# First attention of a fused attention and expert kernel: one VectorE product for both heads, inverse sums in a shared PSUM bank, and k copies moved from ScalarE to VectorE

## The chip, the cores and the metric

The kernel runs on one core of one Trainium2 chip. The metric is the time of the device in microseconds (us), from start to end of one execution, as the median of several runs. The engines are TensorE (PE, with its weight loads as PEld), VectorE (DVE), ScalarE (ACT), GpSimd (POOL) and SyncE (SP), which here only issues DMAs. [...]

## The reference

Attention with global and local keys over 4 batches of 8 heads, 768 positions and 64 columns per head, followed by a mixture of 4 experts over the 3072 rows:

```python
scores = scale * np.matmul(q, k.transpose(0, 1, 3, 2))
scores = scores + bias[None]                 # -slope * distance, per head
scores = np.where(keep, scores, -1e9)        # first 8 keys, and the last 96
a = np.exp(scores - max); a = a / (a.sum(-1) + 1e-9)
x = np.matmul(a, v)                          # rows: 4 * 768, columns: 8 * 64
p = domain_probs / (domain_probs.sum(-1) + 1e-9)
for e in range(4):
    out += p[:, e:e+1] * (np.maximum(x @ w1[e], 0) @ w2[e])
```

## The kernel before

The attention of batch 0 comes first and alone ("first attention", `attention_early`, pools made with `early=True`). The experts of batch 0 then run on PE while the attention of the next batches is woven in, and so on to the end. The change touches the first attention only; the code for the later attention (`early=False`) keeps its form.

The first attention works on four pairs of heads, in the order 0, 2, 1, 3. A pair has six tiles of 128 query rows, so there are 24 tiles, and each call of `flow` (a *step*, numbered 0 to 27 here) takes in one new tile and moves the tiles before it one stage on. For step n the stages are:

- PE: the scores of tiles n and n+1, in even steps, into two PSUM tiles `ps0` and `ps1` (one per head, both tiles beside each other in each);
- DVE and ACT, tile n-1 (`one` in the code): per head, DVE adds the bias and takes the maximum out of PSUM into `pb` (the CUSTOM instruction), and ACT takes the exponential and its row sum `zsum`;
- DVE, tile n-2 (`two`): adds 1e-9 to the two row sums between the two heads of tile n-1, inverts them after the second head (RECIPROCAL), and multiplies `pb` by them, one instruction per head (TENSOR_SCALAR_CACHE_REDUCE, an accumulating form whose sum goes to `spare` and is not used; each is followed by a short READ_ACCUMULATOR);
- PE and ACT, tile n-3: `turn` transposes the scaled `pb` into a PSUM tile `pt`, and ACT copies it to `pT`;
- PE and ACT, in steps 6, 9, 12, ... 27: `weigh` multiplies three turned tiles with v into the PSUM tile `px`, with 20 matmul instructions for tiles 0 to 2 of a pair and 24 for tiles 3 to 5, and ACT copies `px` to `x`.

The first tile of each pair has 128 columns per head, the others 256. After a step, `AHEAD` says whether one more part of a next pair is prepared: three PE transposes of half of q or k into `pt`, and one ACT copy of 384 columns out of it (`prepare_early`). For the last three pairs the k halves come after steps 4, 5, 8, 9, 13 and 14, the q halves after 3, 6, 7, 10, 12 and 15. After the first half of k POOL copies its first 32 columns beside every tile. After steps 17 to 20 DVE has one sum of x blocks each for the experts (`first_sums`, tiles named xB in the trace). After step 25 PE runs a first product of the experts (`opening`, into a `ps` tile), which reads x of the last pair's first half.

All engines take their instructions in the order of the program in this stage (`Ordered.on`), so that an instruction that waits holds up all that is behind it on its engine. Waits follow from the tiles that instructions read and write. [...]

Of the kernel before, what the change touches and what calls it, by code (L numbers as in the profile page):

```python
# [9 lines left out]
F32 = mybir.dt.float32  # L10
# [3 lines left out]
AF = mybir.ActivationFunctionType  # L14
ALU = mybir.AluOpType
# [3 lines left out]
P = 128  # L19
# [167 lines left out]
def attn_moe_kernel(ctx: ExitStack, tc, q, k, v, n_global, n_local, domain_probs, w1, w2, out):  # L187
# [9 lines left out]
    HALF = S // 2  # L197
# [12 lines left out]
    ve, ac, po, sy, te = (Ordered(tc, e) for e in (nc.vector, nc.scalar, nc.gpsimd, nc.sync, nc.tensor))  # L210

    PAIRS = (0, 2, 1, 3)
# [116 lines left out]
    def transpose_half(A, nat, hf):  # L329
        tp = A.pt.tile([P, 512], F32, name="pt")  # L330
        for t in range(TPH):
            te.transpose(tp[:, t * P : (t + 1) * P], nat[:, hf * TPH + t].rearrange("p j d -> p (j d)"), ident)
        return tp
# [30 lines left out]
        if hf == 0:  # L364
            ve.tensor_copy(kd[:, :, :, P:], f32(kd[:, :, 0:1, :NGLOB]).to_broadcast([P, 2, NQT, NGLOB]))

    def prepare_early(A, nat, hf, name, got):

        tp = transpose_half(A, nat, hf)
        tpv = tp[:, :HALF].rearrange("p (t c) -> p t c", c=P)  # L370
        pl = slice(hf * TPH, (hf + 1) * TPH)
        if name == "q":
            if hf == 0:
                got["q"] = A.qd.tile([P, NQT, P], F32, name="early_q")
            ac.activation(got["q"][:, pl, :], tpv, AF.Copy, scale=-SCALE)
            return
        if hf == 0:
            got["k"] = A.kd.tile([P, NQT, PL], F32, name="early_k")
        dst = got["k"]
        ac.copy(dst[:, pl, :P], tpv)  # L380
        if hf == 0:
            po.tensor_copy(dst[:, :, P:], dst[:, 0:1, :NGLOB].to_broadcast([P, NQT, NGLOB]))

# [36 lines left out]
    def softmax(A, new, old):  # L420


        if old:
            pb, zsum = old["pb"], old["zsum"]
        if new:
            t, pr, ps = new["t"], new["pr"], new["ps"]
            cols = slice(0, P) if t == 0 else slice(0, 2 * P)
            bcol = slice(2 * P, 3 * P) if t == 0 else slice(0, 2 * P)
            new["pcol"] = pcol = slice(P, 2 * P) if t == 0 else slice(0, 2 * P)
            nmax = A.small.tile([P, 2], F32, name="nmax")  # L430
            new["zsum"] = A.small.tile([P, 2], F32, name="zsum")
            new["pb"] = A.pb.tile([P, 2, 2 * P], F32, name="pb")
        for j in range(2):
            if new:
                e = new["pb"][:, j, pcol]
                ve.tensor_tensor_reduce(
                    e, ps[j][:, cols], nbias[:, 2 * pr + j, bcol], 1.0, 3.0e38, ALU.add, ALU.min, nmax[:, j : j + 1]
                )
                ac.activation(
                    e, e, AF.Exp, bias=nmax[:, j : j + 1], scale=-1.0, accum_out=new["zsum"][:, j : j + 1]  # L440
                )
            if old:
                if j == 1:
                    ve.reciprocal(zsum, zsum)
                elif A.early:

                    old["spare"] = spare = A.small.tile([P, 3], F32, name="spare")
                    ve.tensor_scalar(zsum, zsum, 1e-9, None, op0=ALU.add, op1=ALU.add, accum_out=spare[:, 2:3])
                else:
                    ac.activation(zsum, zsum, AF.Copy, bias=1e-9)  # L450
        if old:
            for j in range(2):
                p = pb[:, j, old["pcol"]]
                if A.early:
                    ve.tensor_scalar(
                        p, p, zsum[:, j : j + 1], None, op0=ALU.mult, op1=ALU.add, accum_out=old["spare"][:, j : j + 1]
                    )
                else:
                    ac.activation(p, p, AF.Copy, scale=zsum[:, j : j + 1])

    def turn(A, tile_):

        t, pb = tile_["t"], tile_["pb"]
        pt = A.pt.tile([P, 2, 2, P], F32, name="pt")
        pT = A.pT.tile([P, 2, 2, P], F32, name="pT")
        w0 = 1 if t == 0 else 0
        for w in range(w0, 2):
            for j in range(2):
                te.transpose(pt[:, w, j, :], pb[:, j, w * P : (w + 1) * P], ident)
        ac.copy(pT[:, w0:], pt[:, w0:])  # L470
        tile_["pT"] = pT

    def weigh(A, three, x, b):

        px = A.px.tile([P, 512], F32, name=A.pxname)
        for i, tile_ in enumerate(three):
            t, pr, pT = tile_["t"], tile_["pr"], tile_["pT"]
            vt, vg = tile_["v"]["v"], tile_["v"]["vg"]
            for w in range(1 if t == 0 else 0, 2):
                for j in range(2):  # L480
                    vv = vt[:, j, t] if w == 1 else vg[:, j, t - 1]
                    te.matmul(
                        px[j * D : (j + 1) * D, i * P : (i + 1) * P],
                        vv,
                        pT[:, w, j, :],
                        start=(w == 1 if t == 0 else w == 0),
                        stop=(w == 1),
                    )
        cols = slice((t - TPH + 1) * P, (t + 1) * P)
        if x is not None:  # L490
            ac.copy(x[:, pr, cols], px[:, :HALF])
        else:
            piece = A.st.tile([P, HALF], F32, name="piece")
            ac.copy(piece, px[:, :HALF])
            ac.dma_start(xd[b][:, pr, cols], piece)
# [3 lines left out]
    def attention_early(A):  # L499

        b = 0
        x = xs[b] = xp.tile([P, NPAIR, S], F32, name="x")
        tiles, turned, ahead = [None] * 4, [], [None]

        def flow(new=None):

            one, two, three, four = tiles
            if new:
                if new["t"] % 2 == 0:
                    new["ps"], ahead[0] = scores_early(A, new["t"], gots[new["pr"]])  # L510
                else:
                    new["ps"] = ahead[0]
            if four:
                turned.append(four)
            softmax(A, one, two)
            if three:
                turn(A, three)
            if len(turned) == TPH:
                weigh(A, turned, x, b)
                turned.clear()  # L520
            tiles[:] = [new, one, two, three]

        def start(pr):

            nats[pr] = {n: next(load(A, src, b, pr, n)) for n, src in (("q", q), ("k", k), ("v", v))}

        def prepare_all(pr):

            nat, got = nats[pr], gots[pr]
            got["v"] = nat  # L530
            prepare_early(A, nat["q"], 0, "q", got)
            if pr:
                yield 1
            prepare_early(A, nat["k"], 0, "k", got)
            yield 1
            nat["vg"] = windows(A, nat["v"])
            prepare_early(A, nat["k"], 1, "k", got)
            yield 1
            prepare_early(A, nat["q"], 1, "q", got)
            yield 1  # L540

        nats, gots = {}, [{} for _ in range(NPAIR)]
        halves = [load(A, src, b, 0, n, 2) for n, src in (("q", q), ("k", k))]
        bias = biases(start_stack.enter_context(tc.tile_pool(name="setup", bufs=1)))
        next(bias)
        nats[0] = dict(zip(("q", "k"), (next(h) for h in halves)))
        for h in halves:
            next(h)
        nats[0]["v"] = next(load(A, v, b, 0, "v"))
        todo = [prepare_all(pr) for pr in PAIRS]  # L550
        next(bias)
        next(todo[0])
        start(PAIRS[1])
        for m, pr in enumerate(PAIRS):
            cur = gots[pr]
            for t in range(NQT):
                if t == 2 and m + 2 < NPAIR:
                    start(PAIRS[m + 2])
                flow({"t": t, "pr": pr, **cur})
                if (m, t) in BIASES:  # L560
                    next(bias)
                for _ in range(AHEAD[m][t]):
                    while todo and next(todo[0], 0) == 0:
                        todo.pop(0)
                yield
        while any(tiles):
            flow()
            yield
# [281 lines left out]
    late = []  # L850
# [119 lines left out]
    with ExitStack() as start_stack:  # L970
        A = Pools(start_stack, "start", st=1, kd=2, qd=2, nat=2, natv=3, pb=4, ps=2, pt=3, px=1, early=True)
# [11 lines left out]
    op = main.enter_context(tc.tile_pool(name="op", bufs=1))  # L983
# [3 lines left out]
    A = Pools(  # L987
        att_stack, "att", st=1, kd=1, qd=2, nat=1, natv=1, pb=2, ps=2, pt=2, px=0, early=False, side="right"
    )
# [463 lines left out]
```

## Time and profile before

| | us |
|---|---|
| median of 3 runs | 1165.45 (1165.42 to 1165.84) |
| profiled execution, its own time | 1164.69 |
| its span in the profile | 1162.9 |
| busy in the span: PE / DVE / ACT / POOL | 1140.5 / 853.2 / 618.2 / 606.6 |
| PEclk over the span | 0.999 of full speed |
| last copy of x of the first attention starts | 59.98 |

The profile counts times from the start of the span. A row of the timeline gives the start, the duration, the engine and the tiles written and read; where one instruction starts before the one ahead of it has ended, the distance from start to start is what it costs its engine.

### The profile page before, as it was taken

To read this page: it belongs to the slowest core of one execution; us is meant where nothing else is said; L and a number is where in the kernel's file an instruction comes from. 1 tells how busy PE (TensorE), PEld (TensorE's weight loads), DVE (VectorE), ACT (ScalarE), POOL (GpSimd) and SP (SyncE) were. 2 spreads that over 40 slices of the span, in tenths; PEclk is the share of its full clock that TensorE was granted. 3 is DMA by queue.
4 is the path that set the end of the run, shared out by engine and by line. 5 is a ranking of instruction groups with operands and counts; after the bars stand their busy time and mean duration, and the time that the engine had idled before them with its cause. 6 is when DMAs were issued, how large, how long until landed. Compare 5 with 4: busy or idle time off the path is not lost.

```text
span 1162.9 us, 21146 instructions
## 1 busy us (share of the span) xinstructions
PE 1140.5 (98%) x7474; PEld 1062.6 (91%) x7474; DVE 853.2 (73%) x1944; ACT 618.2 (53%) x1597; POOL 606.6 (52%) x592
## 2 busy tenths in 40 slices
PE   7899999999999999999999999999999999999997
PEld 5678898989888989899998899999999999999997
DVE  7977776767767777776776777777777777777776
ACT  6854767777653665655565334444445444444443
POOL 5676645554343314222222327777778855555554
PEclk9999999999999999999999999999999999999999
DMA  9558798778775889978868668888887687777764
GB/s 185 149 172 290 268 294 258 269 253 255 247 261 206 282 269 286 282 234 279 257 196 288 207 215 304 306 302 300 284 314 281 240 303 239 249 247 247 245 232 131
DMA packets 181744, 294.32 MB, mean 253 GB/s; under 512 B 86400, under 2 KB 137088, under 8 KB 169344
## 3 DMA queue, kind: packets, MB, share of 16 engines
q1 hardware_dynamic: 177600, 286.61, 75.0%
q10 hardware_dynamic: 4032, 6.30, 1.5%
q8 instruction: 61, 1.00, 0.4%
q14 instruction: 51, 0.42, 0.1%
HBM read 207.93 MB, written 70.78 MB: 240 GB/s over the span
## 4 chain that ended last, share of the span: by engine, by line
PE 87%; DVE 5%; ACT 3%; POOL 2%; DMA 1%; issue 1%; DVEq 0%; ACTq 0%; POOLq 0%
PE pm L43 36%; PE pf L43 19%; PE X L43 11%; PE Y L43 9%; PE pt L43 7%; PE ps L43 4%; ACT pb L43 1%; DVE pb L43 1%; POOL w1s L43 1%; PE px L43 1%; DVE acc L43 1%; DVE xB L43 1%; DMA x_last<-piece 0%; DVE hA L43 0%; DVE pm L43 0%
## 5 line engine op out<-in xcount | busy, mean ns | idle before, releaser
L43 PE MATMUL pm<-w2s,h 128*128 128x512 f32 x1152 | 282.8, 395 | 3.6 <-DVE h L43 2.6
L43 PEld LDWEIGHTS pm<-w2s,h 128*128 128x128 f32 x1152 | 210.7, 188 | 46.5 <-DVE h L43 4.5
L43 ACT ACTIVATE hf<-pf 128x384 f32<-128x384 f32 x128 | 62.8, 491 | 248.3 <-DVE pf L43 247.1
L43 POOL TENSOR_TENSOR hS<-sf,hS 128x384 fp32r<-128x384 f32 x126 | 134.3, 1084 | 113.0 <-ACT hS L43 112.2
L43 DVE SCALAR_TENSOR_TENSOR acc<-pm,prob,acc 128x512 f32<-128x512 f32 x180 | 132.4, 748 | 54.5 <-PE pm L43 53.6
L43 POOL TENSOR_TENSOR sums<-raw 128x256 f32<-128x256 f32 x54 | 39.2, 745 | 211.8 <-DMA raw<-in_moe_w_dram 133.4
L43 PE MATMUL pm<-xT,w1s 128*128 128x384 f32 x744 | 147.9, 341 | 0.0
L43 PE MATMUL pf<-xT,w1s 128*128 128x384 f32 x768 | 146.5, 335 | 0.9 <-ACT hf L43 0.7
L43 PEld LDWEIGHTS pf<-xT,w1s 128*128 128x128 f32 x768 | 131.4, 188 | 1.7 <-ACT hf L43 1.2
L43 PEld LDWEIGHTS pm<-xT,w1s 128*128 128x128 f32 x744 | 128.0, 188 | 0.7 <-issue 0.7
L43 ACT ACTIVATE pb<-pb,nmax 128x256 f32<-128x256 f32 (+1 forms) x192 | 94.2, 498 | 58.1 <-DVE nmax L43 54.2
L43 DVE TENSOR_TENSOR hA<-hf,hA 128x384 fp32r<-128x384 f32 x94 | 84.6, 925 | 50.6 <-ACT hA L43 49.1
L43 PE MATMUL pm<-xB,w1s 128*128 128x384 f32 x574 | 116.8, 344 | 0.1
L43 PE MATMUL pf<-xB,w1s 128*128 128x384 f32 x576 | 110.7, 335 | 0.2 <-ACT hf L43 0.2
L43 PEld LDWEIGHTS pm<-xB,w1s 128*128 128x128 f32 x574 | 99.9, 188 | 5.5 <-issue 1.4
L43 ACT ACTIVATE h<-pm 128x384 fp32r<-128x384 f32 x128 | 62.0, 490 | 74.4 <-DVE pm L43 73.3
L43 PEld LDWEIGHTS pf<-xB,w1s 128*128 128x128 f32 x576 | 98.7, 188 | 0.6 <-ACT hf L43 0.4
L43 POOL TENSOR_TENSOR sf<-hf 128x384 f32<-128x384 f32 x63 | 70.3, 1116 | 43.6 <-ACT hf L43 43.6
L43 DVE CUSTOM_DVE_ANT_0 pb<-ps,nbias 128x256 f32<-128x256 f32 (+1 forms) x192 | 72.3, 395 | 5.8 <-PE ps L43 4.8
L43 DVE SCALAR_TENSOR_TENSOR h<-pm,h 128x384 fp32r<-128x384 f32 x128 | 69.5, 550 | 8.4 <-ACT h L43 6.8
L43 PE MATMUL Y<-w2b,hS 128*128 128x256 f32 x576 | 74.0, 282 | 0.0
L43 PE MATMUL X<-w2b,hS 128*128 128x256 f32 x576 | 73.9, 282 | 0.0
(159 smaller groups left out, 2183.5 us busy)
## 6 DMA issues: line engine op xcount, KB each, us to landing
w1s<-kept SPq DMA_DIRECT2D x47, 1792.0 KB, 8.2
w2b<-kept SPq DMA_DIRECT2D x224, 256.0 KB, 4.3
kept<-w1s SPq DMA_DIRECT2D x16, 1792.0 KB, 7.3
raw<-in_moe_w_dram SPq DMA_DIRECT2D x43, 512.0 KB, 4.7
kept<-w2s SPq DMA_DIRECT2D x16, 1024.0 KB, 6.9
w2s<-kept SPq DMA_DIRECT2D x16, 1024.0 KB, 5.5
qd<-qd SPq DMA_DIRECT2D x48, 192.0 KB, 3.2
v<-in_v_dram SPq DMA_DIRECT2D x16, 384.0 KB, 4.1
```

Source lines behind the costliest of these rows:

```text
L43: ins = fn(*args, **kwargs)
```

## The change

Three things change in the first attention.

- The `px` bank is allocated once (`A.bank`). `weigh` uses its first 384 columns; four columns behind them (`A.inverse`, two for even and two for odd tiles) hold the inverse row sums, which RECIPROCAL now writes there, to PSUM, and no longer in place in SBUF.
- One `tensor_tensor` product multiplies both heads of a tile (512 columns, or 256 for the first tile of a pair) by the inverse sums, read from PSUM with a broadcast. The two accumulating products and their sums go.
- For the last three pairs DVE, not ACT, copies the two halves of k out of `pt`.

```diff
-        ac.copy(dst[:, pl, :P], tpv)
+        (ve.tensor_copy if late else ac.copy)(dst[:, pl, :P], tpv)
...
-                if j == 1:
+                if j == 1 and A.early:
+                    inverse = A.inverse[:, old["t"] % 2]
+                    ve.reciprocal(inverse, zsum)
+                elif j == 1:
                     ve.reciprocal(zsum, zsum)
...
-        if old:
+        if old and A.early:
+            p = pb[:, :, old["pcol"]]
+            ve.tensor_tensor(p, inverse.unsqueeze(2).to_broadcast(list(p.shape)), p, op=ALU.mult)
+        elif old:
             for j in range(2):
                 p = pb[:, j, old["pcol"]]
-                if A.early:
-                    ve.tensor_scalar(
-                        p, p, zsum[:, j : j + 1], None, op0=ALU.mult, op1=ALU.add, accum_out=old["spare"][:, j : j + 1]
-                    )
-                else:
-                    ac.activation(p, p, AF.Copy, scale=zsum[:, j : j + 1])
+                ac.activation(p, p, AF.Copy, scale=zsum[:, j : j + 1])
...
-        px = A.px.tile([P, 512], F32, name=A.pxname)
+        px = A.bank[:, :HALF] if A.early else A.px.tile([P, 512], F32, name=A.pxname)
...
+        A.bank = A.px.tile([P, 512], F32, name="px")
+        A.inverse = A.bank[:, HALF : HALF + 4].rearrange("p (t j) -> p t j", j=2)
...
-            prepare_early(A, nat["k"], 0, "k", got)
+            prepare_early(A, nat["k"], 0, "k", got, pr in PAIRS[1:])
...
-            prepare_early(A, nat["k"], 1, "k", got)
+            prepare_early(A, nat["k"], 1, "k", got, pr in PAIRS[1:])
```

## Rows read from the trace of the kernel before

**Rows 1.** Busy time by stretch (us): PE, PEld, DVE, ACT, POOL, PEclk, DMA.

```profile
17.30:41.30 24.00, 23.59 (x227) 17.80 (x224) 22.00 (x144) 23.96 (x81) 13.74 (x18) 1.00 0.77 183
41.30:57.20 15.90, 12.25 (x112) 8.48 (x112) 15.58 (x90) 12.45 (x40) 12.94 (x15) 1.00 0.49 137
74.00:110.00 36.00, 35.88 (x194) 33.45 (x195) 26.57 (x48) 16.83 (x35) 30.77 (x30) 1.00 0.87 296
150.00:300.00 150.00, 149.59 (x924) 135.19 (x919) 108.71 (x269) 109.45 (x295) 80.04 (x82) 1.00 0.80 262
```

**Rows 2.** Timeline of DVE, one full step: start us, us, engine, line, operation.

```profile
50.70 0.42 DVE L43 CUSTOM_DVE_ANT_0 pb<-ps,nbias 128x256 f32<-128x256 f32 x1
...
51.05 0.15 DVE L43 TENSOR_SCALAR_CACHE_REDUCE zsum<-zsum 128x2 f32<-128x2 f32 x1
...
51.12 0.42 DVE L43 CUSTOM_DVE_ANT_0 pb<-ps,nbias 128x256 f32<-128x256 f32 x1
...
51.47 0.16 DVE L43 RECIPROCAL zsum<-zsum 128x2 f32<-128x2 f32 x1
51.66 0.48 DVE L43 TENSOR_SCALAR_CACHE_REDUCE pb<-pb,zsum 128x256 f32<-128x256 f32 x1
...
52.47 0.42 DVE L43 CUSTOM_DVE_ANT_0 pb<-ps,nbias 128x256 f32<-128x256 f32 x1
```

**Rows 3.** Timeline of DVE: products of 128 columns, sums of 384, start of step 20's.

```profile
47.93 0.34 DVE L43 TENSOR_SCALAR_CACHE_REDUCE pb<-pb,zsum 128x128 f32<-128x128 f32 x1
...
48.21 0.34 DVE L43 TENSOR_SCALAR_CACHE_REDUCE pb<-pb,zsum 128x128 f32<-128x128 f32 x1
...
48.47 0.55 DVE L43 TENSOR_TENSOR xB<-x,xB 128x384 f32<-128x384 f32 x1
65.39 0.55 DVE L43 TENSOR_TENSOR u<-pm,p 128x384 f32<-128x384 f32 x1
65.86 0.55 DVE L43 SCALAR_TENSOR_TENSOR h<-pm,h 128x384 fp32r<-128x384 f32 x1
73.99 0.74 DVE L43 TENSOR_SCALAR acc<-pm,prob 128x512 f32<-128x512 f32 x1
```

**Rows 4.** Timeline: a PSUM tile written in two parts, read in the first.

```profile
7.73 0.80 PE L43 MATMUL ps<-early_k,early_q 64*128 64x128 f32 x4 [0.57 <-ACT early_k L43]
8.32 1.06 PE L43 MATMUL ps<-early_k,early_q 64*128 64x256 f32 x4
9.42 0.29 DVE L43 CUSTOM_DVE_ANT_0 pb<-ps,nbias 128x128 f32<-128x128 f32 x1 [1.78 <-PE ps L43]
121.51 0.63 PE L43 MATMUL ps<-kd,qd 128*128 128x256 f32 x4
122.18 0.43 DVE L43 CUSTOM_DVE_ANT_0 pb<-ps,nbias 128x256 f32<-128x256 f32 x1 [0.66 <-PE ps L43]
```

**Rows 5.** Timeline: the last weigh, step 27, from PE over ACT to DVE.

```profile
57.87 0.60 PE L43 MATMUL pt<-ident,pb 128*128 128x128 f32 x4
58.40 0.44 PE L43 MATMUL px<-pT,vg 128*64 128x128 f32 x4
59.98 0.48 ACT L43 COPY x<-px 128x384 f32<-128x384 f32 x1 [0.83 <-PE px L43]
60.49 0.56 DVE L43 TENSOR_TENSOR xB<-x 128x384 f32<-128x384 f32 x1 [3.22 <-ACT x L43]
```

**Rows 6.** Timeline of DVE and PE around the k transposes of steps 4 and 5.

```profile
16.90 0.42 DVE L43 CUSTOM_DVE_ANT_0 pb<-ps,nbias 128x256 f32<-128x256 f32 x1
17.14 0.49 PE L43 MATMUL pt<-ident,k 128*128 128x128 f32 x3
17.98 0.55 PE L43 MATMUL pt<-ident,k 128*128 128x128 f32 x3
18.66 0.42 DVE L43 CUSTOM_DVE_ANT_0 pb<-ps,nbias 128x256 f32<-128x256 f32 x1
```

**Rows 7.** Timeline: weigh of step 18, and the DVE product of that step.

```profile
41.28 1.31 DVE L43 TENSOR_TENSOR xB<-x 128x384 f32<-128x384 f32 x1
41.90 0.44 PE L43 MATMUL px<-pT,v 128*64 128x128 f32 x4
43.87 0.47 DVE L43 TENSOR_SCALAR_CACHE_REDUCE pb<-pb,zsum 128x256 f32<-128x256 f32 x1
```

**Rows 8.** Timeline of ACT: a k copy, and the instruction behind it.

```profile
34.40 0.59 ACT L43 COPY early_k<-pt 128x384 f32<-128x384 f32 x1
34.77 0.63 ACT L43 ACTIVATE pb<-pb,nmax 128x256 f32<-128x256 f32 x1
```

More of the change, by code (lines that the diff above doesn't have):

```diff
@@ L365, in prepare_k, with prepare_early @@
             ve.tensor_copy(kd[:, :, :, P:], f32(kd[:, :, 0:1, :NGLOB]).to_broadcast([P, 2, NQT, NGLOB]))
-    def prepare_early(A, nat, hf, name, got):
+    def prepare_early(A, nat, hf, name, got, late=False):
         tp = transpose_half(A, nat, hf)
@@ L442, in softmax @@
             if old:
-                if j == 1:
+                if j == 1 and A.early:
+                    inverse = A.inverse[:, old["t"] % 2]
+                    ve.reciprocal(inverse, zsum)
+                elif j == 1:
                     ve.reciprocal(zsum, zsum)
                 elif A.early:
-                    old["spare"] = spare = A.small.tile([P, 3], F32, name="spare")
-                    ve.tensor_scalar(zsum, zsum, 1e-9, None, op0=ALU.add, op1=ALU.add, accum_out=spare[:, 2:3])
+                    spare = A.small.tile([P, 1], F32, name="spare")
+                    ve.tensor_scalar(zsum, zsum, 1e-9, None, op0=ALU.add, op1=ALU.add, accum_out=spare)
                 else:
                     ac.activation(zsum, zsum, AF.Copy, bias=1e-9)
-        if old:
+        if old and A.early:
+            p = pb[:, :, old["pcol"]]
+            ve.tensor_tensor(p, inverse.unsqueeze(2).to_broadcast(list(p.shape)), p, op=ALU.mult)
+        elif old:
             for j in range(2):
                 p = pb[:, j, old["pcol"]]
-                if A.early:
-                    ve.tensor_scalar(
-                        p, p, zsum[:, j : j + 1], None, op0=ALU.mult, op1=ALU.add, accum_out=old["spare"][:, j : j + 1]
-                    )
-                else:
-                    ac.activation(p, p, AF.Copy, scale=zsum[:, j : j + 1])
+                ac.activation(p, p, AF.Copy, scale=zsum[:, j : j + 1])
     def turn(A, tile_):
```

## The prediction

> **What bounds the kernel now.** I read the page for shares, then the busy time by stretch, then the timelines of the first attention, engine by engine. From 74 us on PE is busy all but without a gap (35.88 of 36 us, 149.59 of 150) [rows 1]: what the first attention gains or loses moves the rest as a block, so all of the change is to be read in the first 60 us. There two engines take turns. From 17.3 to 41.3 ACT works 23.96 of 24.00 us, with DVE close behind at 22.00; from 41.3 to 57.2 DVE works 15.58 of 15.90 [rows 1]. PE has room in both. ACT is what the k copies leave, DVE is where they go.
>
> One full step costs DVE, from start to start [rows 2]: 0.35 (first CUSTOM), 0.07 (the 1e-9), 0.35 (second CUSTOM), 0.19 (RECIPROCAL), 0.81 (two products), in all 1.77 us. The first tile of a pair is shorter: its products take 0.27 each [rows 3], and its CUSTOM lasts 0.29 and not 0.42 [rows 4, 2], which is 0.13 less per head. Steps 6 to 17 took DVE from 18.66 [rows 6] to 41.28 [rows 7], 22.62 us. Their work is 12 x 1.77 less 2 x 0.53 for two first tiles (0.27 in products, 0.26 in CUSTOMs), 20.2 us; so DVE waited 2.4 us there, for ACT.
>
> **The product.** Two products of 256 cost 0.40 to 0.41 each, two of 128 cost 0.27 each [rows 2, 3]: 0.13 for 128 columns. A sum of two tensors over 384 columns takes 0.47 from start to start, with one operand in PSUM (65.39 to 65.86) as with both in SBUF (the 0.55 long one at 48.47 has the same length) [rows 3]. For 512 columns I take 0.47 + 0.13 = 0.60. Bounds: 4 x 0.13 = 0.53 below, 0.74 above, the whole length of the 512 column scaling out of PSUM [rows 3]. I keep 0.60, as its two nearest rows are of its own kind. It saves 0.21 a tile, 24 times.
>
> **The reciprocal** writes two columns to PSUM. No row shows that. I take the old 0.19 (reading from PSUM cost nothing extra above), with 0.14 more as the upper bound, the distance of 0.74 from 0.60; a gain of more than its 0.19 cannot be.
>
> **The k copies.** ACT loses six copies of 0.37 (34.40 to 34.77) [rows 8], 2.2 us, all in its full stretch. DVE gets six of 384 columns out of PSUM: 0.47 by the sums above, 0.27 below (a product of 128 columns), since no copy of this kind is in the trace; I take 0.47. The copy also waits for PE's three transposes, and on DVE everything of the next step is queued behind it. After step 4 those transposes run at 17.14 and end at 17.63, while DVE was free at 16.90 [rows 6], and at 16.3 with three cheaper products. So DVE copies from 17.68 to 18.15, does step 5 in 1.56 (19.7) and copies again (transposes done at 18.53), and begins step 6 at 20.2 instead of 18.66 [rows 6]: **+1.5 us**, the saved products included.
>
> **The shared bank.** This decides. The inverse sums now lie in the tile that PE writes and ACT reads in each weigh. Do waits go by tile or by columns? Rows 4 show a PSUM tile written in two parts. The first tile's scores run from 7.73 for 0.80 us; DVE needs only them, but starts at 9.42, when the second tile's scores beside them have ended (8.32 + 1.06 = 9.38). The later attention does the same: four matmuls, two per head, run from 121.51 to 122.14, and DVE's first head starts at 122.18, after both. So I take it that waits go by the whole tile.
>
> [...]
>
> By tile, step n with a weigh becomes a chain. The product of step n reads the bank, so PE may start the weigh only after it; ACT copies x after PE; the reciprocal of step n+1 writes the bank, so it waits for ACT. Before, the weigh of step 18 began at 41.90, two us ahead of that step's second product (43.87) [rows 7], and DVE waited for none of it. Behind the waiting reciprocal are queued the product and both CUSTOMs of the next step; ACT's exponentials and PE's transposes wait for these.
>
> The length of the chain: from the first px instruction (58.40) over ACT to DVE's next instruction (60.49) is 2.09 us for 24 matmuls [rows 5]. Add 0.08, by which a 0.55 us product outlasts its 0.47, and 0.05 for the hand-over (0.04 at 122.14): 2.2. With 20 matmuls it is 0.26 less (58.40 to 59.98 is 1.58; 1.58 / 24 x 4): 1.95. In that time DVE has only its own 0.77 of CUSTOMs and 1e-9 to do, or 0.51 for the first tile of a pair. So it stands idle:
>
> - steps 6 and 12 (20 matmuls, a first tile next): 1.95 - 0.51 = 1.45 each;
> - steps 15 and 21 (24 matmuls): 2.2 - 0.77 = 1.43 each;
> - step 18: 1.95 - 0.51 - 0.47 for a sum of x blocks in between = 0.97;
> - step 24: no new tile, only the 1e-9, 0.07 of work: 1.88;
> - step 9: the k copy stands ahead of the CUSTOMs, and its transposes behind the weigh on PE: 0.13 + 1.58 + 0.49 [rows 6] = 2.2 idle, then copy, CUSTOMs and a reciprocal that finds x done.
>
> Together 10.8 us.
>
> **The sum** from step 6 to the last product: 20 products -4.2; four k copies +1.9; idle time by the bank +10.8; the old waits for ACT -2.4, since DVE is now behind ACT. That is +6.1, and with the start **+7.6 us**. The last transposes stand behind the opening product on PE, which starts with x of step 24 and moves along, so nothing is added there. ACT's saved 2.2 us buy nothing here, as ACT then waits for DVE. On the profiled execution's own time, 1164.69, this is 1172.3; its time lies 0.76 below the median of 1165.45, so on the median it is 1173.0. SP and POOL keep their instructions and order; POOL's copy of k's first columns only follows DVE in place of ACT.
>
> Bounds of this case: the product -1.4 to +2.8 (20 x -0.07 and +0.14), the reciprocal 0 to +2.8, the k copies -1.2 to 0, the seven gaps 0.2 each either way (1.4), the old waits up to +2.4 if they stay. All of it carries on by rows 1; if the weights' loads and POOL catch up meanwhile, I allow a loss of a quarter, -1.9. They will not all fall on one side; half of them gives +4 to +12, so 1169.5 to 1177.5.
>
> **The rivals.**
>
> - *Waits go by columns, faster.* Then no chain forms. DVE in steps 6 to 17 has 20.2 - 12 x 0.21 + 4 x 0.47 = 19.6 us, starts 1.5 later and ends at 39.8 instead of 41.28; eight more products give 1.7. That is -3.2 at best. If the k copies' waits for PE keep returning and ACT keeps pacing DVE (its 24 us of work fall only to 21.8), it is 0. Middle -1.6: 1163.9. It decides if the reciprocals after a weigh don't wait for ACT. For it: the columns are disjoint. Against it: rows 4. Chance 0.12.
> - *Only PE waits.* The weigh is held up to the product, but the reciprocal isn't held by x. PE loses about 1 us at a weigh, of which its free time in the step takes most; the start's +1.5 stays, the product and ACT give back a part. 0 to +3, about 1167. Chance 0.08.
> - *PSUM operands are dear.* The product takes 0.74 and the reciprocal 0.33: 7.6 + 2.8 + 2.8, about 1178.5. Against it: the equal 0.55 of rows 3. Chance 0.05.
> - That the change doesn't do what it says: two products become one for certain, so it has no case of its own.
>
> **How the numbers follow.** My case has a chance of 0.75, and the forecast is its 1173.0. This kernel's measurement can tell about 0.2% from no change, 2.3 us: 1163.1 and 1167.8. Slower: nearly all of my case (0.73), 0.05, and 0.02 of the second rival: 0.80. Faster: half of the first rival, 0.06. No change: the rest, 0.14. For 8 in 10 the range takes in my case but for its thin ends and goes down over the second rival: 1165.5 to 1177.5.
>
> **What would show it.** Right: seven RECIPROCALs that write to px with 1 to 2 us of idle DVE before them, ended by ACT's x (that of step 9 at the k copy instead, ended by PE); the px loads of PE ended by DVE; 24 TENSOR_TENSORs on pb of about 0.68 us; ACT no longer full before 41 us; the last x copy near 67.5. Wrong: RECIPROCALs that follow the CUSTOMs at once; a product of over 0.75; a step 6 that begins at 18.7 or earlier; or a stage that ends 7 us late while the end of the kernel doesn't.

## The result and the profile after

The changed kernel took 1175.64 us (median of 4 runs, 1173.24 to 1176.31), the kernel before 1165.43 beside it (4 runs). The ratio is 1.0088, with a 95% interval of 1.0076 to 1.01: slower, by 10.2 us. The forecast was 1173.0 in a range of 1165.5 to 1177.5. The profiled execution took 1176.31 us, with a span of 1174.5; before it was 1164.69 and 1162.9.

Busy time by stretch of the changed kernel, with the columns of [rows 1], and two single microseconds among them:

```profile
17.30:41.30 24.00, 18.70 (x176) 14.11 (x175) 17.61 (x86) 17.93 (x58) 10.12 (x13) 1.00 0.65 148
41.30:57.20 15.90, 9.70 (x95) 6.89 (x93) 13.18 (x61) 11.26 (x37) 11.34 (x14) 1.00 0.41 90
57.20:74.00 16.80, 13.80 (x104) 10.36 (x105) 7.60 (x32) 8.17 (x24) 5.32 (x6) 0.80 0.27 95
74.00:110.00 36.00, 35.15 (x164) 28.97 (x163) 29.16 (x53) 17.30 (x33) 30.20 (x27) 1.00 0.76 242
150.00:300.00 150.00, 149.18 (x954) 134.85 (x953) 108.67 (x264) 109.23 (x289) 76.62 (x78) 1.00 0.81 260
...
59.00:60.00 1.00, 1.00 (x10) 0.67 (x8) 0.00 (x0) 0.26 (x1) 0.92 (x2) 0.50 0.94 258
66.00:67.00 1.00, 1.00 (x14) 1.00 (x12) 0.00 (x0) 0.00 (x0) 0.00 (x0) 0.50 0.00 0
```

The reader is to see two things. No engine bounds the first attention any more: from 17.3 to 41.3 ACT falls from 23.96 to 17.93 us, DVE from 22.00 to 17.61, PE from 23.59 to 18.70 [rows 1]. Less work is done in the same time because the engines wait for each other. And from 57.2 to 74.0 the granted clock is 0.80 of full speed: in the single microseconds 59 and 66 it is 0.50. Before, it was 1.00 from 57.2 to 74.0 too, and 0.999 over the span.

The waits of the changed kernel from 8 to 70 us (engine and what it works on, what it waited for: us in total, times, longest):

```profile
PE px L43 <- DVE pb L43: 10.4, 7, 2.0
DVE px L43 <- ACT x L43: 9.8, 6, 2.7
ACT x L43 <- PE px L43: 9.5, 7, 2.0
```

This is a ring. PE's weigh waits for DVE's product, ACT's x for PE's weigh, DVE's next reciprocal for ACT's x, once per weigh (after the weigh of step 9 DVE's copy of k stands first, and waits for PE). The timeline of the changed kernel shows it link by link (start, us, engine, operation, idle time before it and what ended it):

```profile
18.02 0.56 DVE L43 COPY early_k<-pt 128x384 f32<-128x384 f32 x1 [1.59 <-PE pt L43]
...
20.52 0.41 DVE L43 CUSTOM_DVE_ANT_0 pb<-ps,nbias 128x256 f32<-128x256 f32 x1
...
21.49 0.69 DVE L43 TENSOR_TENSOR pb<-px,pb 128x512 f32<-128x512 f32 x1
...
22.09 0.28 DVE L43 CUSTOM_DVE_ANT_0 pb<-ps,nbias 128x128 f32<-128x128 f32 x1
...
22.23 0.44 PE L43 MATMUL px<-pT,v 128*64 128x128 f32 x4 [1.31 <-DVE pb L43]
...
23.59 0.48 ACT L43 COPY x<-px 128x384 f32<-128x384 f32 x1 [0.98 <-PE px L43]
...
24.10 0.17 DVE L43 RECIPROCAL px<-zsum 128x2 f32<-128x2 f32 x1 [1.43 <-ACT x L43]
...
26.80 0.56 DVE L43 COPY early_k<-pt 128x384 f32<-128x384 f32 x1 [0.40 <-PE pt L43]
...
28.99 0.44 PE L43 MATMUL px<-pT,vg 128*64 128x128 f32 x4 [2.00 <-DVE pb L43]
...
31.04 0.56 DVE L43 COPY early_k<-pt 128x384 f32<-128x384 f32 x1 [2.10 <-PE pt L43]
...
38.24 0.18 DVE L43 RECIPROCAL px<-zsum 128x2 f32<-128x2 f32 x1 [1.36 <-ACT x L43]
...
40.48 0.42 DVE L43 TENSOR_TENSOR pb<-px,pb 128x256 f32<-128x256 f32 x1
...
40.94 0.56 DVE L43 COPY early_k<-pt 128x384 f32<-128x384 f32 x1
...
45.21 0.17 DVE L43 RECIPROCAL px<-zsum 128x2 f32<-128x2 f32 x1 [1.39 <-ACT x L43]
...
51.96 0.17 DVE L43 RECIPROCAL px<-zsum 128x2 f32<-128x2 f32 x1 [0.96 <-ACT x L43]
...
55.20 0.41 PE L43 MATMUL pt<-ident,pb 128*128 128x128 f32 x2 [1.56 <-DVE pb L43]
...
57.61 0.44 PE L43 MATMUL px<-pT,vg 128*64 128x128 f32 x4 [2.00 <-DVE pb L43]
...
59.58 1.27 POOL L43 TENSOR_TENSOR w1s<-sums,w1s 128x512 fp32r<-128x512 f32 x1
...
59.63 2.08 PE L43 MATMUL ps<-early_k,early_q 64*128 64x256 f32 x8
...
60.25 0.17 DVE L43 RECIPROCAL px<-zsum 128x2 f32<-128x2 f32 x1 [1.94 <-ACT x L43]
...
60.46 0.69 DVE L43 TENSOR_TENSOR pb<-px,pb 128x512 f32<-128x512 f32 x1
...
65.44 0.70 PE L43 MATMUL px<-pT,v 128*64 128x128 f32 x4 [1.26 <-DVE pb L43]
...
68.40 0.17 DVE L43 RECIPROCAL px<-zsum 128x2 f32<-128x2 f32 x1 [2.70 <-ACT x L43]
...
72.08 0.48 ACT L43 COPY x<-px 128x384 f32<-128x384 f32 x1 [0.83 <-PE px L43]
```

Read 21.49 to 24.10 as one turn of the ring: product, weigh, copy of x, reciprocal. Before, a weigh could begin ahead of its step's products [rows 7]. Now the weigh begins once the product is done, and DVE stands idle for 1.43 us. The last copy of x starts at 72.08 and no longer at 59.98 [rows 5], 12.1 later; the span is 11.6 longer. From there on the rest moves as a block, with PE busy 35.15 of 36 and 149.18 of 150 us: from the last copy of x to the end of the span it is 1102.4 us, against 1102.9 before.

Groups of DVE instructions of the changed kernel from 8 to 70 us, by shape (count, busy us, mean ns, idle time ahead of them):

```profile
L43 DVE TENSOR_TENSOR pb<-px,pb 128x512 f32<-128x512 f32 x20 | 13.8, 691 | 0.7
...
L43 DVE RECIPROCAL px<-zsum 128x2 f32<-128x2 f32 x24 | 4.1, 170 | 9.8 <-ACT x L43 9.8
```

The product itself is as cheap as was taken: 0.69 us long, 0.60 from start to start (21.49 to 22.09). The price of the shared bank is idle time: the 9.8 us of the second row, and the 2.10 ahead of the copy of k at 31.04.

### The profile page after: what moved, and what is told of

It is laid out like the page before. It is cut to its first block, busy times and chain, and to the rows that moved or that the text cites. A ratio compares the mean times of both kernels' runs of the same rounds, so it can differ in the third digit from the quotient of the medians.

```text
span 1174.5 us, 21083 instructions
## 1 busy us (share of the span) xinstructions
PE 1142.7 (97%) x7474; PEld 1064.9 (91%) x7474; DVE 850.3 (72%) x1878; ACT 618.9 (53%) x1591; POOL 607.6 (52%) x592
## 4 chain that ended last, share of the span: by engine, by line
PE 90%; DVE 5%; ACT 2%; POOL 1%; issue 1%; DMA 1%; ACTq 0%; DVEq 0%
PE pm L43 40%; PE pf L43 19%; PE X L43 11%; PE Y L43 9%; PE pt L43 7%; PE ps L43 4%; DVE pb L43 1%; PE px L43 1%; DVE xB L43 0%; DVE hA L43 0%; POOL w1s L43 0%; ACT pb L43 0%; DVE acc L43 0%; DMA out_dram<-acc 0%; POOL xB L43 0%
```

## The experiments

Ten kernels were run, in three groups. What is compared is the ratio to the kernel before, whose runs beside them had medians of 1164.8 (19 runs, first to fourth kernel), 1164.4 (25 runs, fifth to eighth) and 1165.26 (10 runs, the last two).

**1. The k copies back on ACT.** From the changed kernel:

```diff
-            prepare_early(A, nat["k"], 0, "k", got, pr in PAIRS[1:])
+            prepare_early(A, nat["k"], 0, "k", got)
...
-            prepare_early(A, nat["k"], 1, "k", got, pr in PAIRS[1:])
+            prepare_early(A, nat["k"], 1, "k", got)
```

> The changed kernel, with all k copies back on ScalarE. Bank theory (the reciprocal waits for the copy of x, the weigh for the product): the seven idle times of VectorE ahead of a reciprocal stay, the 1.5 us at the start and the wait of step 9 go; 1169.5 to 1172, ratio 1.004 to 1.0055, last x copy at 65.5 to 68.5 us. Rival k theory (the loss is VectorE standing behind the k transposes): 1165 or less, ratio 1.000 or below, last x copy at 60 or earlier.

Measured: 1171.94 us, ratio 1.0066 (1.005 to 1.0083). The loss stays without the k copies on DVE: in its waits DVE's reciprocals wait 9.3 us for ACT's x, seven times. The copies' share is the difference of the two ratios, 0.0022 or some 2.6 us (3.7 by the medians); the two intervals overlap, so it is an estimate.

**2. The bank alone.** From the kernel before: only the reciprocal writes into the px bank, and the two old products read their scalars there.

```diff
-                if j == 1:
+                if j == 1 and A.early:
+                    inverse = A.inverse[:, old["t"] % 2]
+                    ve.reciprocal(inverse, zsum)
+                elif j == 1:
                     ve.reciprocal(zsum, zsum)
...
-                        p, p, zsum[:, j : j + 1], None, op0=ALU.mult, op1=ALU.add, accum_out=old["spare"][:, j : j + 1]
+                        p, p, inverse[:, j : j + 1], None, op0=ALU.mult, op1=ALU.add, accum_out=old["spare"][:, j : j + 1]
...
-        px = A.px.tile([P, 512], F32, name=A.pxname)
+        px = A.bank[:, :HALF] if A.early else A.px.tile([P, 512], F32, name=A.pxname)
```

> The kernel before, with one thing changed: the reciprocal writes to four columns of the px bank, and the two old accumulating products read their scalars from there; k stays on ScalarE. Bank theory: this alone gives the loss, 1172 to 1176, ratio 1.006 to 1.009, reciprocals idle 1 to 2.7 us behind the copy of x. Rival (the product, the k copies or the planner's order cost the time): 1165 to 1167, no idle time ahead of the reciprocals.

Measured: 1174.97 us, ratio 1.0091 (1.0074 to 1.0108), as slow as the whole change. The waits of this kernel from 8 to 70 us:

```profile
DVE px L43 <- ACT x L43: 11.0, 7, 2.8
ACT x L43 <- PE px L43: 10.2, 7, 3.0
...
PE px L43 <- DVE pb L43: 8.8, 5, 2.8
```

The same ring, in a kernel with the old products and ACT's old copies. Two values per row and step, written to another place, cost some 10 us.

**3. The product alone, inverse sums in SBUF.** From the kernel before, with no shared bank and the k copies on ACT:

```diff
+        if old and A.early:
+            p = pb[:, :, old["pcol"]]
+            ve.tensor_tensor(p, zsum.unsqueeze(2).to_broadcast(list(p.shape)), p, op=ALU.mult)
```

> The kernel before, with one product for both heads, but the inverse sums in SBUF; k stays on ScalarE. Bank theory: no chain, VectorE saves 0.2 us a tile where it paces the stage; 1163.5 to 1165.5, last x copy at 58 to 59.5 us. Rival (a product with two SBUF operands is held up by GpSimd, as the 1.31 us of one sum of x blocks may be): products over 1 us between 33 and 56 us, 1165.5 to 1168.

Measured: 1166.74 us (10 runs), ratio 1.0019 (1.0009 to 1.003). There is no gain from the product, so the rival of the expectation came. Its groups by shape:

```profile
L43 DVE TENSOR_TENSOR pb<-zsum,pb 128x512 f32<-128x512 f32 x20 | 16.2, 808 | 0.7
```

The same product takes 0.81 on the mean where both operands lie in SBUF, against 0.69 with one in PSUM (the `px` tile). Two products of its timeline show the difference, with what POOL did beside the first:

```profile
56.00 1.26 POOL L43 TENSOR_TENSOR w2s<-raw,w2s 128x512 fp32r<-128x512 f32 x1
...
56.08 1.73 DVE L43 TENSOR_TENSOR pb<-zsum,pb 128x512 f32<-128x512 f32 x1
...
58.69 0.69 DVE L43 TENSOR_TENSOR pb<-zsum,pb 128x512 f32<-128x512 f32 x1
```

Beside POOL's sum of two SBUF tensors the product takes 1.73, 1.04 more; with POOL out of the way (0.00 busy from 58 to 59) it takes 0.69. With the inverse in PSUM, all 20 products have a mean of 691 ns, and the changed kernel's product at 60.46 takes 0.69 beside POOL's sum of 59.58. What holds the product up beside POOL isn't shown further. By these rows PSUM was a sound place for the inverse; the bank that it was put in was not. (The granted clock was 0.79 from 41.3 to 57.2 in this profile, whose execution took 1168.62, so a part of the loss may be the clock's. But the six runs with a mean clock of 0.998 have a median of 1165.85, and the seven of the kernel before at 0.998 beside them 1164.83.)

**4. The k copies on DVE alone.** From the kernel before:

```diff
-        ac.copy(dst[:, pl, :P], tpv)
+        (ve.tensor_copy if late else ac.copy)(dst[:, pl, :P], tpv)
```

> The kernel before, with only the k copies of the last three pairs on VectorE. Bank theory: no long idle times, only VectorE's waits for the k transposes at steps 4 and 5 (about 1.5 us) against 2.2 us that ScalarE saves; 1165 to 1168, last x copy at 60 to 62.5 us. Rival k theory: most of the loss, 1170 or more.

Measured: 1166.03 us (10 runs), ratio 1.0014 (1.0005 to 1.0024), some 1.6 us (1.2 by the medians).

**5. The whole change with a bank of its own for the inverse sums.** The px bank holds only them; the weigh takes its tile from the three buffers of `pt`, eight buffers in all as before (four of `ps`, three of `pt`, one of `px`).

```diff
-        px = A.bank[:, :HALF] if A.early else A.px.tile([P, 512], F32, name=A.pxname)
+        px = A.pt.tile([P, 512], F32, name="pt") if A.early else A.px.tile([P, 512], F32, name=A.pxname)
```

> The changed kernel, but weigh takes its PSUM tile from the three buffers of the transposes, so that the inverse sums have the old px bank for themselves. Bank theory: the idle times ahead of the reciprocals go; what stays is VectorE's wait for the k transposes and perhaps a lower granted clock, as when only the k copies moved; 1164 to 1167, ratio 0.999 to 1.002. Rival (PSUM operands are dear, or the planner's order of the rest costs it): 1170 or more.

Measured: 1162.11 us (10 runs), ratio 0.9983 (0.9973 to 0.9992): faster than before, below the range that I had given, and some 12 us faster than the change by the two ratios. Its groups of DVE, by shape:

```profile
L43 DVE TENSOR_TENSOR pb<-px,pb 128x512 f32<-128x512 f32 x20 | 13.8, 692 | 0.7
...
L43 DVE RECIPROCAL px<-zsum 128x2 f32<-128x2 f32 x24 | 4.0, 168 | 0.0
...
L43 DVE COPY early_k<-pt 128x384 f32<-128x384 f32 x6 | 3.3, 554 | 1.7 <-PE pt L43 1.5
```

The idle time ahead of the reciprocals is gone, the product is unchanged, and the last copy of x starts at 58.53. The granted clock is 1.00 in all stretches up to 74 us.

**6. The control.** The kernel before with that px line of the fifth kernel alone, so that its old px bank lies unused.

> The kernel before, with weigh's PSUM tile taken from the three buffers of the transposes and one bank left idle: the control for the own bank. 1164.5 to 1166.5 if three buffers do for both; up to 1168 if transposes wait for buffers.

Measured: 1165.41 us (10 runs), ratio 1.0008 (0.9998 to 1.0018), no difference that can be told. So the fifth kernel's gain is not the other pool's. Nor is it the clock's alone: of the 25 runs of the kernel before beside them, the 12 whose mean clock was 0.999 have a median of 1164.01, 1.9 above the fifth kernel, whose ten runs had 0.998 to 1.0.

**7. PE kept busy ahead of each weigh.** The changed kernel with 12 transposes of the identity, whose result nothing reads, so that PE doesn't stand idle while it waits for the product.

```diff
+        if A.early:
+            fill = A.pt.tile([P, 4, P], F32, name="pt")
+            for n in range(12):
+                te.transpose(fill[:, n % 4], ident, ident)
```

> The changed kernel, with 12 transposes of the identity that nobody reads on TensorE ahead of each weigh, into a buffer of the transposes; they take about 1.3 us that TensorE otherwise waits for the product. [...] Rival (the clock does not follow TensorE's idle times, or its low stretches hide behind VectorE): same clock pattern, or same time, 1175 to 1177.

The rival stands against the clock theory: PE's idle times bring the lower clock, and that is a part of the loss. For it I had put 1172 to 1174.5 us, with the last copy of x at 69 to 71.

Measured: 1174.49 us, ratio 1.0088 (1.0071 to 1.0105). The mean clock is 0.999 in each of its four runs, against 0.993 to 0.998 in the changed kernel's, and 1.00 in all stretches up to 74 us. But the filler ahead of the last weigh lies on the path itself: in its timeline ACT waits 2.14 for that weigh, against 0.83 in the changed kernel.

```profile
64.86 0.17 DVE L43 RECIPROCAL px<-zsum 128x2 f32<-128x2 f32 x1 [1.94 <-ACT x L43]
...
69.43 0.48 ACT L43 COPY x<-px 128x384 f32<-128x384 f32 x1 [2.14 <-PE px L43]
```

The last gap falls from 2.70 to 1.94, but the filler ahead of the last weigh costs 1.31 (2.14 less 0.83), and the median can't be told from the changed kernel's: for the time, the run is inconclusive.

**8. Its own bank, k copies on ACT.** The fifth kernel with the first's edit.

> As the own bank version, with k copies back on ScalarE: only the one product, with inverse sums in a bank that no other engine uses. Bank theory: products at 0.69 us without GpSimd's hold-ups, no long idle times; 1163 to 1165.5, at best the version that beats both. Rival: 1166 or more, by waits for transpose buffers or a clock that falls.

Measured: 1161.8 us (10 runs), ratio 0.998 (0.9971 to 0.999). It beats both kernels, the one before by 2.6 us, and lies below the range that I had given.

**9. Its own bank, k of the last two pairs on DVE.** The fifth kernel with `PAIRS[2:]` in place of `PAIRS[1:]`.

> The own bank version with the k copies of the last two pairs alone on VectorE (steps 8, 9, 13, 14), those of steps 4 and 5 on ScalarE. If the k copies cost by VectorE's wait for the transposes at the start (step 6 late by about 1.5 us), this is the better split: 1160.5 to 1162, last x copy 0.5 to 1.5 us ahead of the version with all k copies on ScalarE. Rival (ScalarE and VectorE pace the stage together, so moving the copies gives nothing): as the versions with all k copies on either engine, 1161.5 to 1162.5.

Measured: 1161.62 us (7 runs), ratio 0.9976 (0.9965 to 0.9987). Kernels 5, 8 and 9 can't be told apart: with the one product and without the ring, it makes no measured difference which engine copies k (with the old products it cost some 1.6 us, experiment 4).

**10. The filler, but not ahead of the last weigh.** From the changed kernel:

```diff
+        if A.early and len(three) == TPH and not (three[0]["pr"] == PAIRS[-1] and three[0]["t"] == TPH):
+            fill = A.pt.tile([P, 4, P], F32, name="pt")
+            for n in range(12):
+                te.transpose(fill[:, n % 4], ident, ident)
```

> The changed kernel with the 12 unread transposes ahead of each weigh but the last, where they only delay it. Clock theory: granted clock 1.00 up to 74 us, last x copy at 67.5 to 68.5 us, as the sum of idle times by the bank gives without a lower clock; 1172 to 1174. Rival (the last x copy stays above 69.5): a part of the lost time has another cause than bank and clock.

Measured: 1173.27 us, ratio 1.0068 (1.0051 to 1.0085). Its last copy of x starts at 69.69, past the rival's line of 69.5: by what I had set down, a part of the lost time has another cause than the bank's idle times and the clock. The sum further below names most of it. The same two single microseconds of this kernel:

```profile
59.00:60.00 1.00, 1.00 (x16) 0.78 (x14) 0.00 (x0) 0.45 (x2) 0.92 (x3) 1.00 0.88 268
66.00:67.00 1.00, 1.00 (x7) 0.74 (x6) 0.55 (x2) 0.84 (x2) 0.00 (x0) 1.00 0.00 0
```

And its timeline:

```profile
59.44 1.13 PE L43 MATMUL ps<-early_k,early_q 64*128 64x256 f32 x8
...
60.06 0.17 DVE L43 RECIPROCAL px<-zsum 128x2 f32<-128x2 f32 x1 [1.39 <-ACT x L43]
...
63.14 1.47 PE L43 MATMUL pt<-ident 128*128 128x128 f32 x12
...
63.48 0.69 DVE L43 TENSOR_TENSOR pb<-px,pb 128x512 f32<-128x512 f32 x1
...
64.55 0.44 PE L43 MATMUL px<-pT,v 128*64 128x128 f32 x4
...
66.42 0.17 DVE L43 RECIPROCAL px<-zsum 128x2 f32<-128x2 f32 x1 [1.93 <-ACT x L43]
...
69.69 0.48 ACT L43 COPY x<-px 128x384 f32<-128x384 f32 x1 [0.83 <-PE px L43]
```

With the clock at full speed the eight score matmuls take 1.13 and not 2.08, and the last two gaps are 1.39 and 1.93 and not 1.94 and 2.70. Up to the gap of step 18 (51.96 in the changed kernel, 52.38 here) the fillers have made this kernel 0.42 later; at the last copy of x it is 2.39 earlier. So the lower clock cost the changed kernel's profiled execution some 2.8 us, by the comparison of one execution of each. It may be 0.3 more, as the filler at 63.14 ends at 64.61 and holds up its weigh (64.55), whose product ended at 64.17. All four runs of this kernel had a mean clock of 0.999; but the two kernels' intervals overlap, so what the clock costs in the median is not settled.

## Why the prediction was right, and which terms were mis-sized

**The bank.** Right, and the cause of the loss. Waits go by the whole tile, as read from [rows 4]: the second experiment has the loss with the bank alone (ratio 1.0091), and with a bank of its own, in the fifth, it is gone (0.9983). (Bank and tile are one here, `A.bank`: which of the two the wait goes by isn't shown, nor whether it is needed where the columns are disjoint.) The product's gain and the cost of the k copies, some 2 to 3 us each by experiments 1, 4 and 8, about cancel. The seven idle times, each forecast against measured in the changed kernel: step 6, 1.45 and 1.43; step 9, 2.2 and 2.10; step 12, 1.45 and 1.36; step 15, 1.43 and 1.39; step 18, 0.97 and 0.96; step 21, 1.43 and 1.94; step 24, 1.88 and 2.70. The first five hold within 0.1. The last two are 0.51 and 0.82 too small, by the clock.

**The clock, a term that is missing.** The forecast priced PE's matmuls by rows of the kernel before at full speed all along. The ring makes PE stand idle too, and it came to 58 us with 9.70 of 15.90 us of work in the stretch before, against 12.25 [rows 1]. After it had stood idle for 1.56 and 2.00, with 0.41 of work between (the rows of 55.20 and 57.61), its clock fell to 0.50, and again after the 1.26 of 65.44. That the idle times have a part in the falls is shown by experiments 7 and 10, where PE is given work in them and the clock stays at 1.00. But an idle time by itself doesn't decide it: ahead of the weigh of step 9 PE stood idle for 2.00 too (the row of 28.99), and the clock stayed at 1.00.

**The sum at the last copy of x**, 7.6 forecast against 12.1 in the profile. The clock makes 2.8 of the difference. The start makes 0.36: step 6 begins at 20.52, 1.86 and not 1.5 after the old start of 18.66, as the copy of step 4 starts at 18.02 and not at 17.68. The k copy after step 8 waits 0.40 for PE's transposes, which I had costed at nothing. And a pair's first tile, with products of 256 columns, was priced like the others: the one of 40.48 takes 0.46 from start to start against 0.54 for the two that it replaces, 0.08 saved and not 0.21, another 0.13. That is 3.7 of 4.5; the remaining 0.8 lies in small pieces that I haven't followed singly.

Of the median's 1175.64 the forecast lacks only 2.6. In the profiled executions 0.5 of the 12.1 is given back by the end, and their difference of 11.6 is 1.4 above that of the medians, as the change's took 0.7 more than its median and that of the kernel before 0.7 less. So it is partly luck that 2.6 is about the clock's share: it is what is left of 4.5. The range held, but its bounds had no term for the clock; what made room for it were costs of the product and of the reciprocal that didn't come. The tenth kernel, with the clock at full speed, has a median of 1173.27.

**The product.** 0.60 from start to start, as taken; the reciprocal to PSUM takes 0.170 against 0.159 before. The rival of dear PSUM operands is out. **The k copies** cost 0.47 each as taken (40.94 to 41.41), and as a whole some 2 us, by experiments 1 and 4: that edit alone makes the kernel slower. By the prediction's terms it would be +1.5 at the start, with the 0.2 of step 5's cheaper product put back, +1.9 for the four later copies and -2.4 for the old waits for ACT: 1.2, where experiment 4 has 1.6 by its ratio and 1.2 by the medians.

**The rivals.** Waits by columns: out, by the row of 24.10 alone. Only PE waits: out, as six reciprocals wait for ACT's x, and the copy of step 9 for PE. Of the signs that I named as right, the seven idle times came, though two lie outside 1 to 2 us (0.96 and 2.70), and ACT is far from full before 41 us. The products of 0.69 are 20 and not 24, as the first tiles have 256 columns, and the last copy of x came at 72.08 and not near 67.5.

**Left open.** What the lower clock costs in each execution. The changed kernel's four runs took 1176.31, 1175.09, 1176.19 and 1173.24 us at mean clocks of 0.996, 0.994, 0.993 and 0.998: the run with the highest is the shortest, the others don't follow that order. Open too is what, beside the idle time, decides whether the clock falls.

## What to carry to other kernels

Before a few values are put into a corner of a PSUM bank that another engine writes, ask who reads and writes that tile next: here the wait did not go by columns, and the engines that share it were tied into one ring, with DVE idle for 9.8 us behind it (ratio 1.0091 with the bank alone). An operand in PSUM can still be the right choice for DVE, if it has a bank that only DVE uses: here the product kept its 0.69 so, and the ratio was 0.9983. And when a new wait makes PE stand idle, price the matmuls behind it at the lower clock as well, as a bound: here it was 0.50 for some 3 us, twice, and cost some 2.8 us of 12.1.

## What was not expected of the hardware

TensorE's clock fell to 0.50 for some 3 us, twice (0.71, 0.50, 0.50 and 0.58 in the microseconds from 58 to 62; 0.62, 0.50, 0.50 and 0.67 from 65 to 69), after idle times of 2.00 and 1.26 us; it cost some 2.8 us, since PE's matmuls were on the path there. The same idle time need not bring a fall. In the kernel before and in the sixth experiment PE stands idle for the same 1.51 us ahead of the same transposes:

```profile
48.43 0.50 PE L43 MATMUL pt<-ident,pb 128*128 128x128 f32 x2 [1.51 <-DVE pb L43]
...
48.84 0.51 PE L43 MATMUL pt<-ident,pb 128*128 128x128 f32 x2 [1.51 <-DVE pb L43]
```

Behind the first, of the kernel before, the granted clock from 50 to 51 us is 1.00; behind the second, of the sixth experiment, it is 0.50. What makes the difference isn't shown. The kernel before may have such falls in other executions than the profiled one: over the three groups its runs with a mean clock of 0.997 have a median of 1165.07 (17 runs), those with 0.999 one of 1164.22 (21 runs), though in the third group alone the order is the other way (3 runs and 4).

A product of two SBUF operands on DVE took 0.69 us with POOL idle, and up to 1.73 beside POOL's sums (experiment 3).

At the very start, executions differ whatever the kernel: the third group of eight score matmuls, from 14 to 17 us, takes 2.08 us in the profiles of before, after, and experiments 9 and 10, and 1.13 in those of experiments 1 to 8, though the granted clock reads 1.00 from 14 to 17 us in either kind. So times of the last copy of x are subtracted above only between profiles of one kind (after, before and 10). The cause stays open.
